# Halo and weight loads in pieces, and a second PSUM bank for the input transposes, in a dilated causal convolution

## The chip, the cores and the metric

The kernel runs on one core of a Trainium2 chip. The metric is the device time of one execution in microseconds (us). An execution has two numbers: its measured time, and the span of the profile (first to last instruction), which is shorter by about 1.75 us in the kernel before and by about 2.0 us in the changed kernel. Positions inside a kernel are given in us from the start of the span.

Names: the matrix engine is PE (PEld is its weight load), VectorE is DVE, ScalarE is ACT, GpSimd is POOL, the engine that issues transfers is SP. PSUM is the memory that the matrix engine writes its results to (`ps` in the profiles); the kernel uses it as eight banks. Copying a result out of it is called an eviction here.

## The reference

```python
B, T, D, K = 2, 16000, 144, 15            # x: B,T,D   w: K,D,2D   w_o: D,D   bf16
dil = 2; pad = (K - 1) * dil
xp = jnp.pad(x, ((0, 0), (pad, 0), (0, 0)))
h = sum over i of einsum('btc,cd->btd', xp[:, pad - i*dil : pad - i*dil + T, :], w[i])   # condensed
f, g = h[..., :D], h[..., D:]
return (tanh(f) * sigmoid(g)) @ w_o
```

It is a causal convolution with 15 taps at a distance of 2, a gate, and a projection.

## The kernel before

Each of the 128 partitions holds 125 consecutive time steps of one batch, plus a halo of 30 earlier rows that belong to the partition before it. Transposes on the matrix engine bring the channels onto the partitions, ScalarE copies them out of PSUM into a ring (`RX`), and VectorE forms three sums and differences per row (`RM`), from which two output rows are made together with fewer products. The transformed weights (`FW`) are made on the chip too. A main loop of 126 pairs of rows follows. The parts that the change and the argument touch are these:

```python
XTP = PS[:, 4, :].bitcast(BF16).rearrange("p (t h c) -> p t h c", t=4, h=2)   # one PSUM bank

def load_x_halo(b):                       # 30 rows, one piece: 112 + 15 partitions; row 0 is zero
    # ...
    S.add("pool", lambda e: [e.memset(XN[0:1, 0:HALO, :], 0.0)], writes=[("xn", "hz")], name="halo_z")
    S.add("sp", lambda e: [e.dma_start(XN[1:113, 0:HALO, :], xv[b][0:112, J - HALO:J, :])],
          writes=[("xn", "h0")], dma=k0, name="halo0")
    S.add("sp", lambda e: [e.dma_start(XN[113:128, 0:HALO, :], xv[b][112:127, J - HALO:J, :])],
          writes=[("xn", "h1")], dma=k1, name="halo1")
# ... compact(): POOL copies the last 16 channels of the rows into XRP

def op_prep(b, tq):                       # one group of four rows
    # PE: four transposes of XN into XTP, and from the fourth group on four of XRP ("packed rows")
    S.add("pe", emit_tx, reads=rk, writes=[("xtp",)], name="tx")
    # ACT: copy XTP to RX; the next group's transposes wait for it
    S.add("act", emit_cx, reads=[("xtp",)], writes=wk, name="cx")
    # DVE: three operations RX -> RM, one for each of the sums and differences
    # ...

def weight_transforms():                  # ten, three matmuls each, PSUM banks 0 to 3 in turn
    # PE: MB[bank] = I W[3q] +- I W[3q+1] + I W[3q+2]
    # ACT: FW[sgn, q] = 0.5 * MB[bank]
    # ...

load_halo_and_compact(0)
load_chunk_and_compact(0, 0)              # 8 rows
load_weights()                            # W (15 taps), 15 small pieces, w_o
for ci in range(1, NCH):
    load_chunk_and_compact(0, ci)
# ...
for n in init_tq:                         # nine groups
    op_prep(n // NTQ, n % NTQ)
weight_transforms()
for s in range(NP + 2):                   # main loop
    # ...
```

Of the kernel before, what the change touches and what calls it, by code (L numbers as in the profile page):

```python
# [122 lines left out]
def build_kernel(nc, x, w, w_o, out):  # L123
# [30 lines left out]
    r = HALO  # L154
    seq = [8, 16, 32]
    i = 0
    while r < NR:
        s = seq[i] if i < len(seq) else 40
        s = min(s, NR - r)
        chunks.append((r, r + s))  # L160
        r += s
        i += 1
    NCH = len(chunks)

    with ExitStack() as es:
# [22 lines left out]
        n_in_sems = 3 + B * (NCH + 2)  # L188
# [17 lines left out]
        XTP = PS[:, 4, :].bitcast(BF16).rearrange("p (t h c) -> p t h c", t=4, h=2)  # L206
# [23 lines left out]
        def load_x_halo(b):  # L230
            k0 = new_in_slot()
            k1 = new_in_slot()
            S.add("pool", lambda e: [e.memset(XN[0:1, 0:HALO, :], 0.0)], writes=[("xn", "hz")], name="halo_z")
            S.add("sp", lambda e: [e.dma_start(XN[1:113, 0:HALO, :], xv[b][0:112, J - HALO:J, :])],
                  writes=[("xn", "h0")], dma=k0, name="halo0")
            S.add("sp", lambda e: [e.dma_start(XN[113:128, 0:HALO, :], xv[b][112:127, J - HALO:J, :])],
                  writes=[("xn", "h1")], dma=k1, name="halo1")

# [10 lines left out]
        def load_x_chunk(b, ci):  # L249
            lo, hi = chunks[ci]  # L250
            k = new_in_slot()
            S.add("sp", lambda e: [e.dma_start(XN[:, lo:hi, :], xv[b][:, lo - HALO:hi - HALO, :])],
                  writes=[("xn", ci)], dma=k, name="xchunk")

        def load_weights():
            k = new_in_slot()
            S.add("sp", lambda e: [e.dma_start(W[:], w[:, 0:DM, :].rearrange("k c d -> c k d"))],
                  writes=[("w",)], dma=k, name="w")
            k2 = new_in_slot()
            wl = []  # L260
            for q in range(2):
                for g in range(NGP):
                    tap = q * NGP + (NGP - 1 - g)
                    if tap < K:
                        wl.append((q, g, tap))

            def emit_wg(e):
                return [e.dma_start(WG[g * DR:(g + 1) * DR, 0, q, :], w[tap, DM:D, :]) for (q, g, tap) in wl]
            S.add("sp", emit_wg, writes=[("wg", q, g) for (q, g, tap) in wl], dma=k2, ndma=len(wl), name="wg")
            k3 = new_in_slot()  # L270
            S.add("sp", lambda e: [e.dma_start(WO[:, 0, :], w_o[0:DM, :]),
                                   e.dma_start(WO[DM - DR:DM, 1, :], w_o[DM:D, :])],
                  writes=[("wo",)], dma=k3, ndma=2, name="wo")

        def xn_keys(lo, hi):
            ks = []
            if lo < HALO:
                ks += [("xn", "hz"), ("xn", "h0"), ("xn", "h1")]
            for ci, (a, c) in enumerate(chunks):
                if a < hi and lo < c:  # L280
                    ks.append(("xn", ci))
            return ks

        def xr_keys(b, rows):
            ks = set()
            for r_ in rows:
                if r_ < HALO:
                    ks.add(("xr", b, "h", r_ % 2))
                else:
                    for ci, (a, c) in enumerate(chunks):  # L290
                        if a <= r_ < c:
                            ks.add(("xr", b, ci, r_ % 2))
            return sorted(ks, key=str)

        def load_halo_and_compact(b):
            load_x_halo(b)
            compact(b, 0, HALO, xn_keys(0, HALO), "h")

        def load_chunk_and_compact(b, ci):
            load_x_chunk(b, ci)  # L300
            lo, hi = chunks[ci]
            compact(b, lo, hi, [("xn", ci)], ci)

        def weight_transforms():
            outs = []
            for q in range(NQ):
                for sgn in range(2):
                    outs.append((sgn, q))
            for n_, (sgn, q) in enumerate(outs):
                bank = n_ % 4  # L310

                def emit(e, sgn=sgn, q=q, bank=bank):
                    ins = []
                    for k in range(3):
                        idm = IDENT[:, 1, :] if (sgn == 1 and k == 1) else IDENT[:, 0, :]
                        ins.append(e.matmul(MB[bank], lhsT=idm, rhs=W[:, 3 * q + k, :], start=(k == 0), stop=(k == 2)))  # L316
                    return ins
                S.add("pe", emit, reads=[("ident", 0), ("ident", 1), ("w",)], writes=[("mb", bank)], name="wt")
                S.add("act", (lambda sgn=sgn, q=q, bank=bank: lambda e: [e.activation(  # L319
                    out=FW[:, sgn, q, :], in_=MB[bank], func=ACTF.Copy, scale=0.5)])(),  # L320
                    reads=[("mb", bank)], writes=[("fw", sgn, q)], name="wt_ev")
            S.add("act", lambda e: [e.activation(out=WG[:, 1, :, :], in_=WG[:, 0, :, :], func=ACTF.Copy, scale=-1.0)],
                  reads=[("wg", q, g) for q in range(2) for g in range(NGP)], writes=[("wgn",)], name="wgn")
# [4 lines left out]
        def op_prep(b, tq):  # L328
# [6 lines left out]
            sx = g0 % RSX  # L335
            rows_main = [jj0 + t + HALO for t in range(nt)]
# [17 lines left out]
            S.add("pe", emit_tx, reads=rk, writes=[("xtp",)], name="tx")  # L354
# [14 lines left out]
            S.add("act", emit_cx, reads=[("xtp",)], writes=wk, name="cx")  # L369
# [63 lines left out]
        def op_mm(b, ja, gi):  # L433
# [26 lines left out]
            if gi >= 2:  # L460
                rk.append(("w",))
# [115 lines left out]

        load_halo_and_compact(0)
        load_chunk_and_compact(0, 0)
        load_weights()  # L580
        for ci in range(1, NCH):
            load_chunk_and_compact(0, ci)
# [34 lines left out]
        for b in range(1, B):  # L617
            last_read = dict()
            for n in range(NTQT):
                if n // NTQ != b - 1 or firstneed[n] >= NP:  # L620
                    continue
                lo, hi = rows_of_tq(n)
                for key in xn_keys(lo, hi):
                    last_read[key] = max(0, stx[n])
            DELAY = 4
            halo_pi = max(last_read.get(("xn", "hz"), 0), last_read.get(("xn", "h0"), 0)) + DELAY
            loads_at.setdefault(halo_pi, []).append((b, "h"))
            for ci in range(NCH):
                pi = max(last_read.get(("xn", ci), 0) + DELAY, halo_pi)
                loads_at.setdefault(min(pi, NP - 1), []).append((b, ci))  # L630

        for n in init_tq:
            op_prep(n // NTQ, n % NTQ)
            flush_t(100)
        weight_transforms()

        for s in range(NP + 2):
# [3 lines left out]
            if s < NP:  # L641
                for (b, what) in loads_at.get(s, []):
                    if what == "h":
                        load_halo_and_compact(b)
                    else:
                        load_chunk_and_compact(b, what)
# [110 lines left out]
```

## Time and profile before

| | before |
|---|---|
| median time (13 executions) | 496.29 us |
| span of the profiled execution | 495.1 us |
| first transpose | 8.15 us |
| first main matmul (line L466) | 29.80 us |
| from there to the end | 465.3 us |

These lines are from the page of the kernel before: busy time with its share of the span and instruction count, then the chain of work that ended last, by engine.

```profile
PE 473.9 (96%) x4650; PEld 394.5 (80%) x4650; DVE 328.2 (66%) x866; ACT 320.7 (65%) x721; POOL 16.6 (3%) x36
...
PE 95%; ACT 2%; DMA 1%; issue 0%; DVE 0%; SPq 0%; DVEq 0%
```

The matrix engine is the bound. The next fence asks for busy time by stage (the ending is left out); the columns are the stretch, its length, then busy us of each engine with its number of instructions, the granted clock, and the transfer engines' share and rate.

```profile
0.00:8.15 8.15, 0.00 (x1) 0.04 (x2) 0.00 (x0) 1.28 (x1) 5.16 (x11) 1.00 0.78 187
8.15:23.64 15.49, 7.75 (x61) 5.70 (x61) 7.43 (x20) 6.82 (x8) 2.34 (x8) 1.00 0.76 249
23.64:29.80 6.16, 5.94 (x32) 3.84 (x31) 1.24 (x4) 4.62 (x11) 1.96 (x5) 1.00 1.00 385
29.80:488.00 458.20, 458.20 (x4543) 383.80 (x4544) 318.47 (x841) 305.39 (x696) 7.13 (x13) 1.00 0.09 32
```

From 29.80 to 488 us the matrix engine is busy for 458.20 of 458.20 us. Nothing can be won there without taking work from it. Before that there is a prologue of 29.80 us in which it is half idle. The granted clock in these records reads 1.00 here even where matmuls are twice as far apart as later, so the spacing has to be read from the instructions, not from that column.

The prologue in order of time, for the matrix engine (start, length, engine, line, operation, count, and in brackets the idle time before it and what ended it):

```profile
8.15 0.58 PE L348 MATMUL ps<-ident,xn 128*128 128x128 bf16 x4 [8.15 <-DMA xn<-in_x_dram]
9.41 0.61 PE L348 MATMUL ps<-ident,xn 128*128 128x128 bf16 x4 [0.68 <-ACT rx L361]
...
12.07 0.27 PE L348 MATMUL ps<-ident,xn 128*128 128x128 bf16 x1 [0.77 <-ACT rx L361]
...
14.19 0.29 PE L348 MATMUL ps<-ident,xn 128*128 128x128 bf16 x1 [1.10 <-ACT rx L360]
...
23.64 5.94 PE L316 MATMUL ps<-w_sb,ident 128*128 128x288 bf16 x30
29.80 1.39 PE L466 MATMUL ps<-fw_sb,rm 128*128 128x288 bf16 x10 [0.22 <-ACT fw_sb L319]
```

The brackets tell the story: after the halo has landed, each group waits for ScalarE's copy of the group before (0.68 us between small groups, 1.10 between those with packed rows). L348 and L351 are the transposes, L316 the weight transforms. The chain of waits shows the same ping-pong, one step at a time:

```profile
13.12 1.02 ACT rx L360
...
14.19 0.29 PE ps L348
...
15.26 1.02 ACT rx L360
...
28.15 1.52 ACT fw_sb L319 x4
```

It ends in ScalarE's queue of evictions (L319).

### The profile page before, as it was taken

What the parts mean: (1) busy time and instruction counts of PE and PEld (TensorE: products, weight loads), DVE (VectorE), ACT (ScalarE), POOL (GpSimd) and SP (SyncE); (2) the same over time, 40 slices, a digit from 0 to 9 for tenths busy, and PEclk for the clock granted to TensorE, in tenths of its full rate; (3) what the DMA queues carried; (4) which work ended last, traced back from release to release, by engine and by line L of the source; (5) the groups of instructions that cost most, each with busy time, mean ns of one, the idle gap of its engine ahead of it and who ended that gap; (6) DMA issues with size and microseconds to landing.
All of it is one profiled execution on the core that took longest, in us unless ns stands there. A gap on an engine that the chain in (4) does not pass through costs nothing.

```text
span 495.1 us, 11433 instructions
## 1 busy us (share of the span) xinstructions
PE 473.9 (96%) x4650; PEld 394.5 (80%) x4650; DVE 328.2 (66%) x866; ACT 320.7 (65%) x721; POOL 16.6 (3%) x36
## 2 busy tenths in 40 slices
PE   1599999999999999999999999999999999999995
PEld 1478888888888888888888888888888888888884
DVE  1546766676676676886776766766766676676663
ACT  2476666666666666776776666666666666666654
POOL 5150000000000000000000000000000000000000
PEclk9999999999999999999999999999999999999998
DMA  8760020000300000303000000000000000000001
GB/s 208 263 208 3 25 73 25 26 25 1 121 26 25 25 25 24 122 24 113 24 26 15 26 2 25 25 26 25 25 25 3 25 25 25 26 25 8 19 26 39
DMA packets 9008, 22.64 MB, mean 46 GB/s; under 512 B 1166, under 2 KB 3582, under 8 KB 7934
## 3 DMA queue, kind: packets, MB, share of 16 engines
q1 hardware_dynamic: 8956, 21.92, 13.1%
q8 instruction: 36, 0.59, 0.5%
q14 instruction: 16, 0.13, 0.1%
HBM read 12.70 MB, written 9.22 MB: 44 GB/s over the span
## 4 chain that ended last, share of the span: by engine, by line
PE 95%; ACT 2%; DMA 1%; issue 0%; DVE 0%; SPq 0%; DVEq 0%
PE ps L466 75%; PE ps L348 4%; PE ps L351 3%; PE ps L528 3%; PE ps L529 3%; PE ps L502 3%; PE ps L503 3%; DMA xn<-in_x_dram 1%; ACT rx L360 1%; PE ps L316 1%; ACT rx L361 0%; ACT fw_sb L319 0%; ACT zt L506 0%; DVE y L485 0%; ACT sg L489 0%
## 5 line engine op out<-in xcount | busy, mean ns | idle before, releaser
L466 PE MATMUL ps<-w_sb,rm 128*128 128x288 bf16 x1260 | 195.6, 286 | 0.0
L466 PE MATMUL ps<-fw_sb,rm 128*128 128x288 bf16 x1260 | 186.1, 286 | 0.2 <-ACT fw_sb L319 0.2
L466 PEld LDWEIGHTS ps<-w_sb,rm 128*128 128x128 bf16 x1260 | 123.3, 98 | 31.1
L466 PEld LDWEIGHTS ps<-fw_sb,rm 128*128 128x128 bf16 x1260 | 120.3, 98 | 28.1 <-issue 0.5
L489 ACT ACTIVATE sg<-y 128x288 bf16<-128x288 f32 x126 | 55.8, 443 | 99.3 <-DVE y L485 99.3
L506 ACT COPY zt<-ps 128x512 bf16<-128x512 bf16 x126 | 73.9, 586 | 55.1 <-PE ps L503 55.0
L466 PE MATMUL ps<-wg_sb,rx 128*128 128x288 bf16 x504 | 103.0, 286 | 0.0
L401 DVE TENSOR_TENSOR rm<-rx 128x512 bf16<-128x512 bf16 (+2 forms) x236 | 89.0, 408 | 17.0 <-ACT rx L361 10.9
L495 DVE TENSOR_TENSOR z<-tf,sg 128x288 bf16<-128x288 bf16 x126 | 38.8, 308 | 83.1 <-ACT tf L491 83.1
L485 DVE TENSOR_TENSOR y<-pq,ps 128x288 f32<-128x288 f32 x126 | 57.3, 454 | 46.3 <-PE ps L466 45.9
L360 ACT COPY rx<-ps 128x1024 bf16<-128x1024 bf16 x72 | 71.7, 996 | 6.9 <-PE ps L351 6.9
L475 DVE TENSOR_TENSOR pq<-s,ps 128x288 f32<-128x288 f32 x126 | 57.3, 455 | 12.3 <-PE ps L466 6.4
L348 PE MATMUL ps<-ident,xn 128*128 128x128 bf16 x306 | 44.4, 229 | 15.9 <-DMA xn<-in_x_dram 8.1
L481 DVE TENSOR_TENSOR y<-pq,ps 128x288 f32<-128x288 f32 x126 | 56.9, 451 | 3.6
L477 DVE TENSOR_TENSOR pq<-s,ps 128x288 f32<-128x288 f32 x126 | 56.4, 448 | 0.0
L491 ACT ACTIVATE tf<-y 128x288 bf16<-128x288 f32 x126 | 53.7, 426 | 0.0
L536 ACT CAST outb<-ps 128x288 bf16<-128x288 f32 x124 | 50.1, 404 | 0.0
L466 PEld LDWEIGHTS ps<-wg_sb,rx 128*128 128x128 bf16 x504 | 44.9, 98 | 6.3
L471 ACT COPY s<-ps 128x288 f32<-128x288 f32 x126 | 47.8, 379 | 0.0
L348 PEld LDWEIGHTS ps<-ident,xn 128*128 128x128 bf16 x306 | 30.5, 102 | 19.7 <-issue 9.1
L528 PE MATMUL ps<-wo_sb,zt 128*128 128x144 bf16 x252 | 44.3, 226 | 0.7 <-ACT outb L536 0.7
L529 PE MATMUL ps<-wo_sb,zt 128*128 128x144 bf16 x252 | 44.3, 226 | 0.0
(27 smaller groups left out, 290.4 us busy)
## 6 DMA issues: line engine op xcount, KB each, us to landing
out_dram<-outb SPq DMA_DIRECT2D x30, 288.0 KB, 2.1
xn<-in_x_dram SPq DMA_DIRECT2D x2, 1440.0 KB, 7.9
xn<-in_x_dram SPq DMA_DIRECT2D x2, 1152.0 KB, 5.9
xn<-in_x_dram SPq DMA_DIRECT2D x2, 1044.0 KB, 8.4
xn<-in_x_dram SPq DMA_DIRECT2D x2, 945.0 KB, 9.8
xn<-in_x_dram SPq DMA_DIRECT2D x2, 576.0 KB, 4.0
w_sb<-in_w_dram SPq DMA_DIRECT2D x1, 1080.0 KB, 10.1
xn<-in_x_dram SPq DMA_DIRECT2D x2, 288.0 KB, 8.2
```

The costliest lines, as they stand in the source:

```text
L348: ins.append(e.transpose(XTP[:, t, 0, :], XN[:, r_, 0:DM], IDENT[:, 0, :]))
L360: return [e.copy(out=RX[:, sx:sx + nt, :, :], in_=XTP[:, 0:nt, :, :])]
L401: S.add("dve", lambda e: [e.tensor_tensor(out=dst, in0=i0, in1=i1, op=op)], reads=rk_, writes=wk_, name="xf")
L466: ins.append(e.matmul(MB[bank], lhsT=l, rhs=r_, start=(ii == 0), stop=(ii == len(mms) - 1)))
L475: S.add("dve", lambda e: [e.tensor_tensor(out=PQ[:, sb, 0, :], in0=S2[:, sb, :], in1=MB[1], op=ADD)], reads=[("s2", sb), ("mb", 1)], write ...
L477: S.add("dve", lambda e: [e.tensor_tensor(out=PQ[:, sb, 1, :], in0=S2[:, sb, :], in1=MB[1], op=SUB)], reads=[("s2", sb), ("mb", 1)], write ...
L481: S.add("dve", lambda e: [e.tensor_tensor(out=Y[:, sb, 0, :], in0=PQ[:, sb, 0, :], in1=MB[2], op=ADD)], reads=[("pq", sb, 0), ("mb", 2)], ...
L485: S.add("dve", lambda e: [e.tensor_tensor(out=Y[:, sb, 1, :], in0=PQ[:, sb, 1, :], in1=MB[3], op=SUB)], reads=[("pq", sb, 1), ("mb", 3)], ...
L489: S.add("act", lambda e: [e.activation(out=SG[:, sb, :, :], in_=Y[:, sb, :, D:D2], func=ACTF.Sigmoid)], reads=[("y", sb, 0), ("y", sb, 1)] ...
L506: S.add("act", lambda e: [e.copy(out=ZT[:, sb, :, :], in_=ZTP[:, :, :])], reads=[("ztp",)], writes=[("zt", sb)], name="cz")
L528: ins.append(e.matmul(OP[:, t, :], lhsT=ZT[:, sb, 2 * t, :], rhs=WO[:, 0, :], start=True, stop=False))
L529: ins.append(e.matmul(OP[:, t, :], lhsT=ZT[:, sb, 2 * t + 1, :], rhs=WO[:, 1, :], start=False, stop=True))
```

## The change

The intent is to start earlier and to wait less: the first rows come in two pieces of 16 and 14 rows; the transposes get a second PSUM bank; the weights come in two loads (9 and 6 taps), so that six of the ten transforms stand between the seventh and the eighth group; and VectorE takes four of the ten evictions. VectorE also fills row 0 of the second piece with zeros.

```diff
+    while r < HALO:
+        s = min(16, HALO - r)
+        chunks.append((r, r + s, True))
...
-        XTP = PS[:, 4, :].bitcast(BF16).rearrange(...)
+        XTPS = [PS[:, k, :].bitcast(BF16).rearrange(...) for k in (4, 7)]
...
+                S.add("pool" if ci % 2 == 0 else "dve", lambda e: [e.memset(XN[0:1, lo:hi, :], 0.0)], ...)
+                S.add("sp", ... XN[1:113, lo:hi, :] <- xv[b][0:112, J - HALO + lo:J - HALO + hi, :] ...)
+                S.add("sp", ... XN[113:128, lo:hi, :] <- xv[b][112:127, ...] ...)
...
+            xb = (b * NTQ + tq) % 2
+            XTP = XTPS[xb]
...
+            if bank < 2:
+                S.add("act", ... e.activation(out=FW[:, sgn, q, :], in_=MB[bank], func=ACTF.Copy, scale=0.5) ...)
+            else:
+                S.add("dve", ... e.tensor_scalar_mul(out=FW[:, sgn, q, :], in0=MB[bank], scalar1=0.5) ...)
...
+        WSPLIT = 9
+        order0 = list(range(0, NHP)) + [first_main, "w0", "w1", "wg"] + list(range(first_main + 1, NCH))
...
         for i_, n in enumerate(init_tq):
             op_prep(n // NTQ, n % NTQ)
+            if i_ == 6:
+                while nwt < nwt_first:        # six
+                    weight_transform(nwt)
+                    nwt += 1
```

More of the change, by code (lines that the diff above doesn't have):

```diff
@@ L153, in build_kernel @@
     chunks = []
-    r = HALO
+    r = 0
+    while r < HALO:
+        s = min(16, HALO - r)
+        chunks.append((r, r + s, True))
+        r += s
     seq = [8, 16, 32]
@@ L159, in build_kernel @@
         s = min(s, NR - r)
-        chunks.append((r, r + s))
+        chunks.append((r, r + s, False))
         r += s
@@ L163, in build_kernel @@
     NCH = len(chunks)
+    NHP = len([c for c in chunks if c[2]])
     with ExitStack() as es:
@@ L186, in build_kernel @@
         PS = es.enter_context(nc.psum_tensor("ps", [128, 8, 512], F32))
-        n_in_sems = 3 + B * (NCH + 2)
+        n_in_sems = 4 + B * (NCH + NHP)
         sem_in = [es.enter_context(nc.semaphore("in%d" % i)) for i in range(n_in_sems)]
@@ L205, in build_kernel @@
         MB = [PS[:, k, 0:D2] for k in range(4)]
-        XTP = PS[:, 4, :].bitcast(BF16).rearrange("p (t h c) -> p t h c", t=4, h=2)
+        XTPS = [PS[:, k, :].bitcast(BF16).rearrange("p (t h c) -> p t h c", t=4, h=2) for k in (4, 7)]
         ZTP = PS[:, 5, :].bitcast(BF16)[:, 0:512].rearrange("p (t c) -> p t c", t=4)
@@ L228, in build_kernel @@
         S.add("pool", lambda e: [e.memset(WO[0:DM - DR, 1, :], 0.0)], writes=[("woz",)], name="woz")
-        def load_x_halo(b):
-            k0 = new_in_slot()
-            k1 = new_in_slot()
-            S.add("pool", lambda e: [e.memset(XN[0:1, 0:HALO, :], 0.0)], writes=[("xn", "hz")], name="halo_z")
-            S.add("sp", lambda e: [e.dma_start(XN[1:113, 0:HALO, :], xv[b][0:112, J - HALO:J, :])],
-                  writes=[("xn", "h0")], dma=k0, name="halo0")
-            S.add("sp", lambda e: [e.dma_start(XN[113:128, 0:HALO, :], xv[b][112:127, J - HALO:J, :])],
-                  writes=[("xn", "h1")], dma=k1, name="halo1")
         def compact(b, lo, hi, rkeys, tag):
@@ L247, in compact, with load_piece, piece_keys, compact_piece @@
                     reads=rkeys, writes=[("xr", b, tag, k)], name="compact")
-        def load_x_chunk(b, ci):
-            lo, hi = chunks[ci]
-            k = new_in_slot()
-            S.add("sp", lambda e: [e.dma_start(XN[:, lo:hi, :], xv[b][:, lo - HALO:hi - HALO, :])],
-                  writes=[("xn", ci)], dma=k, name="xchunk")
+        def load_piece(b, ci):
+            lo, hi, is_halo = chunks[ci]
+            if is_halo:
+                k0 = new_in_slot()
+                k1 = new_in_slot()
+                S.add("pool" if ci % 2 == 0 else "dve", lambda e: [e.memset(XN[0:1, lo:hi, :], 0.0)],
+                      writes=[("xn", ci, "z")], name="halo_z")
+                S.add("sp", lambda e: [e.dma_start(XN[1:113, lo:hi, :], xv[b][0:112, J - HALO + lo:J - HALO + hi, :])],
+                      writes=[("xn", ci, 0)], dma=k0, name="halo0")
+                S.add("sp", lambda e: [e.dma_start(XN[113:128, lo:hi, :], xv[b][112:127, J - HALO + lo:J - HALO + hi, :])],
+                      writes=[("xn", ci, 1)], dma=k1, name="halo1")
+            else:
+                k = new_in_slot()
+                S.add("sp", lambda e: [e.dma_start(XN[:, lo:hi, :], xv[b][:, lo - HALO:hi - HALO, :])],
+                      writes=[("xn", ci, 0)], dma=k, name="xchunk")
+        def piece_keys(ci):
+            if chunks[ci][2]:
+                return [("xn", ci, "z"), ("xn", ci, 0), ("xn", ci, 1)]
+            return [("xn", ci, 0)]
+        def compact_piece(b, ci):
+            lo, hi, is_halo = chunks[ci]
+            compact(b, lo, hi, piece_keys(ci), ci)
         def load_weights():
-            k = new_in_slot()
-            S.add("sp", lambda e: [e.dma_start(W[:], w[:, 0:DM, :].rearrange("k c d -> c k d"))],
-                  writes=[("w",)], dma=k, name="w")
             k2 = new_in_slot()
@@ L276, in xn_keys @@
             ks = []
-            if lo < HALO:
-                ks += [("xn", "hz"), ("xn", "h0"), ("xn", "h1")]
-            for ci, (a, c) in enumerate(chunks):
+            for ci, (a, c, h_) in enumerate(chunks):
                 if a < hi and lo < c:
-                    ks.append(("xn", ci))
+                    ks += piece_keys(ci)
             return ks
@@ L286, in xr_keys @@
             for r_ in rows:
-                if r_ < HALO:
-                    ks.add(("xr", b, "h", r_ % 2))
-                else:
-                    for ci, (a, c) in enumerate(chunks):
-                        if a <= r_ < c:
-                            ks.add(("xr", b, ci, r_ % 2))
-            return sorted(ks, key=str)
-        def load_halo_and_compact(b):
-            load_x_halo(b)
-            compact(b, 0, HALO, xn_keys(0, HALO), "h")
-        def load_chunk_and_compact(b, ci):
-            load_x_chunk(b, ci)
-            lo, hi = chunks[ci]
-            compact(b, lo, hi, [("xn", ci)], ci)
@@ L304, in weight_transforms @@
-        def weight_transforms():
-            outs = []
-            for q in range(NQ):
-                for sgn in range(2):
-                    outs.append((sgn, q))
-            for n_, (sgn, q) in enumerate(outs):
-                bank = n_ % 4
-                def emit(e, sgn=sgn, q=q, bank=bank):
-                    ins = []
-                    for k in range(3):
-                        idm = IDENT[:, 1, :] if (sgn == 1 and k == 1) else IDENT[:, 0, :]
-                        ins.append(e.matmul(MB[bank], lhsT=idm, rhs=W[:, 3 * q + k, :], start=(k == 0), stop=(k == 2)))
-                    return ins
-                S.add("pe", emit, reads=[("ident", 0), ("ident", 1), ("w",)], writes=[("mb", bank)], name="wt")
-                S.add("act", (lambda sgn=sgn, q=q, bank=bank: lambda e: [e.activation(
-                    out=FW[:, sgn, q, :], in_=MB[bank], func=ACTF.Copy, scale=0.5)])(),
-                    reads=[("mb", bank)], writes=[("fw", sgn, q)], name="wt_ev")
+                for ci, (a, c, h_) in enumerate(chunks):
+                    if a <= r_ < c:
+                        ks.add(("xr", b, ci, r_ % 2))
@@ new lines, in xr_keys, with weight_transform, emit @@
+            return sorted(ks, key=str)
+        wt_list = []
+        for q in range(NQ):
+            for sgn in range(2):
+                wt_list.append((sgn, q))
+        def weight_transform(n_):
+            sgn, q = wt_list[n_]
+            bank = n_ % 4
+            def emit(e):
+                ins = []
+                for k in range(3):
+                    idm = IDENT[:, 1, :] if (sgn == 1 and k == 1) else IDENT[:, 0, :]
+                    ins.append(e.matmul(MB[bank], lhsT=idm, rhs=W[:, 3 * q + k, :], start=(k == 0), stop=(k == 2)))
+                return ins
+            S.add("pe", emit, reads=[("ident", 0), ("ident", 1), ("w", 0 if 3 * q + 2 < WSPLIT else 1)],
+                  writes=[("mb", bank)], name="wt")
+            if bank < 2:
+                S.add("act", lambda e: [e.activation(out=FW[:, sgn, q, :], in_=MB[bank], func=ACTF.Copy, scale=0.5)],
+                      reads=[("mb", bank)], writes=[("fw", sgn, q)], name="wt_ev")
+            else:
+                S.add("dve", lambda e: [e.tensor_scalar_mul(out=FW[:, sgn, q, :], in0=MB[bank], scalar1=0.5)],
+                      reads=[("mb", bank)], writes=[("fw", sgn, q)], name="wt_ev")
@@ L322, in weight_transforms, with negate_packed_weights @@
+        def negate_packed_weights():
             S.add("act", lambda e: [e.activation(out=WG[:, 1, :, :], in_=WG[:, 0, :, :], func=ACTF.Copy, scale=-1.0)],
@@ L353, in emit_tx @@
                 return ins
-            S.add("pe", emit_tx, reads=rk, writes=[("xtp",)], name="tx")
+            S.add("pe", emit_tx, reads=rk, writes=[("xtp", xb)], name="tx")
             flush_needed(b * NTQ + tq - RSX // 4 + 1)
@@ L368, in op_prep @@
                     rx_owner[(sx + t, 1)] = g0 + t
-            S.add("act", emit_cx, reads=[("xtp",)], writes=wk, name="cx")
+            S.add("act", emit_cx, reads=[("xtp", xb)], writes=wk, name="cx")
             def transform(h, ring, rslots, kind):
@@ L460, in op_mm @@
             if gi >= 2:
-                rk.append(("w",))
+                rk += [("w", 0), ("w", 1)]
             def emit(e):
@@ L576, in req_tq, with load_w @@
             return b * NTQ + (ja + 2 + HM) // 4
-        load_halo_and_compact(0)
-        load_chunk_and_compact(0, 0)
-        load_weights()
-        for ci in range(1, NCH):
-            load_chunk_and_compact(0, ci)
+        WSPLIT = 9
+        def load_w(hf):
+            k = new_in_slot()
+            t0, t1 = (0, WSPLIT) if hf == 0 else (WSPLIT, K)
+            S.add("sp", lambda e: [e.dma_start(W[:, t0:t1, :], w[t0:t1, 0:DM, :].rearrange("k c d -> c k d"))],
+                  writes=[("w", hf)], dma=k, name="w")
+        first_main = NHP
+        order0 = list(range(0, NHP)) + [first_main, "w0", "w1", "wg"] + list(range(first_main + 1, NCH))
+        for it in order0:
+            if it == "w0":
+                load_w(0)
+            elif it == "w1":
+                load_w(1)
+            elif it == "wg":
+                load_weights()
+            else:
+                load_piece(0, it)
+        for ci in range(NCH):
+            compact_piece(0, ci)
         NTQT = B * NTQ
@@ L622, in build_kernel @@
                 lo, hi = rows_of_tq(n)
-                for key in xn_keys(lo, hi):
-                    last_read[key] = max(0, stx[n])
+                for ci, (a_, c_, h_) in enumerate(chunks):
+                    if a_ < hi and lo < c_:
+                        last_read[ci] = max(0, stx[n])
             DELAY = 4
-            halo_pi = max(last_read.get(("xn", "hz"), 0), last_read.get(("xn", "h0"), 0)) + DELAY
-            loads_at.setdefault(halo_pi, []).append((b, "h"))
+            prev = 0
             for ci in range(NCH):
-                pi = max(last_read.get(("xn", ci), 0) + DELAY, halo_pi)
+                pi = max(last_read.get(ci, 0) + DELAY, prev)
+                prev = pi
                 loads_at.setdefault(min(pi, NP - 1), []).append((b, ci))
-        for n in init_tq:
+        nwt = 0
+        nwt_first = 2 * (WSPLIT // 3)
+        for i_, n in enumerate(init_tq):
             op_prep(n // NTQ, n % NTQ)
+            cur_iter[0] = 10 ** 6
             flush_t(100)
-        weight_transforms()
+            cur_iter[0] = -10 ** 6
+            if i_ == 6:
+                while nwt < nwt_first:
+                    weight_transform(nwt)
+                    nwt += 1
+        while nwt < len(wt_list):
+            weight_transform(nwt)
+            nwt += 1
+        negate_packed_weights()
         for s in range(NP + 2):
@@ L642, in build_kernel @@
                 for (b, what) in loads_at.get(s, []):
-                    if what == "h":
-                        load_halo_and_compact(b)
-                    else:
-                        load_chunk_and_compact(b, what)
+                    load_piece(b, what)
+                    compact_piece(b, what)
                 b, ja, va = pairs[s]
```

## The prediction

> **What bounds the kernel.** The matrix engine: 96% busy by the page, 95% of the chain of waits, and 100% busy at full clock from 36 to 488 us in the stage table. Its waits after 30 us add up to 2.7 us, at the end. So about 465.3 us (29.80 to 495.1) is a solid block that this change does not touch; only the prologue before the first main matmul at 29.80 can shrink.
>
> **The prologue before (timeline).** 8.15 us: the whole halo (1.1 MB) has landed. Nine transpose groups ping-pong with ScalarE through one PSUM bank: 1.28 us each for the first three, about 2.14 for the six with packed rows (1.01 matrix engine, then 1.01 copy). 23.6 us: 30 weight-transform matmuls in 5.9 us, mostly 240 ns apart, ScalarE evicting all ten (0.41 each). 29.80: first main matmul, behind the last eviction.
>
> **What the change does.**
> 1. Halo in two pieces. The halo's packets run from 1.8 to 6.8 us; half the bytes are there at 4.4; the semaphore trails the last packet by about 1.2. The first piece should release the matrix engine at about 6.0. The fourth group needs the second piece and its compaction on POOL: about 8.7 (before: 12.07).
> 2. Second transpose bank. Groups with packed rows are paced by ScalarE's copy, 1.05 us rather than 2.14. Groups 4 to 7: matrix engine done at about 12.8, last copy at 13.9 (VectorE's three ring operations, 1.10 a group, just keep step).
> 3. Weights split 9 and 6 taps; six transforms come between groups seven and eight. The first half should land by about 11: no wait. 18 matmuls: 4.3 us at 240 ns, 2.2 at 122. End: 15.3 to 17.0.
> 4. Two more groups, four transforms, evictions shared with VectorE. The tail is copy, copy (1.05 each), three ring operations (1.1), then VectorE's eviction of transform 7 (estimated 0.47 from its other 288-wide PSUM reads), which stands behind those: about 4.6 us after the first six transforms.
>
> First main matmul: 19.9 to 21.9, centre 20.7, so 9.1 us earlier. Extra costs (more load issues, chunk loads about 1.4 us later, a short VectorE fill in the loop) should stay off the path: chunk 1 is compacted at about 21.7 and needed at about 24. In the main loop the second bank buys nothing, as the matrix engine never waits there for ScalarE.
>
> The Trainium skill, "TensorE: Matmul & The Clock Gate", Part 1, says the array runs at half rate until a free-running window of about 3.4 us has been busy. The trace agrees: spacing halved about 5 us after dense work began at 22.8; the earlier transposes (40% issue) ran at 107 ns all along. Whether the denser new transposes (80%) warm it by 12 to 15 us, or only the transforms do, is most of my range.
>
> **Prediction: 487.3 us, 80% range 485.5 to 489.3.** Faster by over 2%: 0.30; within 2%: 0.69; slower by over 2%: 0.01.
>
> **What would show it.** First transpose at about 6.0, fourth group at 8.7, groups then 1.05 us apart; first transform at about 12.7 without a weight wait; first main matmul near 20.7, released by VectorE's eviction; from there to the end still 465.3 us, two pairs per 7.27.
>
> **What would make it wrong.** The pieces landing together: up to 2 us lost at the start, though the second piece governs anyway. The weight half landing after 13 us. A matrix engine still cold at 20 us, or cooled by the gap of about 2 us before the main loop: about 2 us. A wait for chunk 1 in the first pairs. Better than expected: an early warm clock and a shorter tail, giving 485.5.

## The result

The changed kernel took 487.91 us (median of 8 executions, 487.01 to 488.47) against 496.29 us before (13 executions). The ratio is 0.9829, 95% interval 0.9818 to 0.9839: faster, by less than 2%. A ratio is the mean time of one kernel's runs over that of the other's in the same rounds, so it is not quite the ratio of these medians. Executions over 1.5% slower than the fastest of the same kernel are left out of the means. The predicted time was 487.3 us.

| | before | after | predicted |
|---|---|---|---|
| median time | 496.29 | 487.91 | 487.3 |
| span of the profiled execution | 495.1 | 486.1 | |
| first transpose | 8.15 | 5.82 | 6.0 |
| fourth group (first with packed rows) | 12.07 | 8.91 | 8.7 |
| first weight transform | 23.64 | 12.79 | 12.7 |
| first main matmul | 29.80 | 20.15 | 20.7 |
| from there to the end | 465.3 | 465.95 | 465.3 |

The page of the changed kernel, the same two lines:

```profile
PE 471.3 (97%) x4650; PEld 393.3 (81%) x4650; DVE 331.3 (68%) x872; ACT 318.7 (66%) x717; POOL 15.5 (3%) x40
...
PE 96%; DMA 1%; DVE 1%; ACT 1%; SPq 0%; issue 0%; POOL 0%; POOLq 0%; DVEq 0%
```

The stages of the changed kernel, cut at its own first transpose, first transform, first main matmul and ending (left out):

```profile
0.00:5.82 5.82, 0.01 (x1) 0.04 (x2) 0.90 (x1) 1.28 (x1) 3.48 (x11) 1.00 0.68 189
5.82:12.79 6.97, 5.24 (x44) 4.31 (x45) 4.09 (x12) 4.25 (x6) 2.13 (x6) 1.00 0.86 213
12.79:20.15 7.36, 5.67 (x48) 4.17 (x47) 5.71 (x18) 5.88 (x11) 0.83 (x2) 1.00 0.60 189
20.15:479.10 458.95, 458.50 (x4543) 383.64 (x4544) 319.51 (x842) 304.77 (x694) 9.05 (x21) 1.00 0.11 40
```

The two middle stages, 8.15 to 29.80 us before, have shrunk from 21.65 to 14.33 us, and the first by 2.33 us. The loop stage is now busy for 458.50 of 458.95 us: there is a hole of 0.45 us that was not there before.

The matrix engine's prologue after:

```profile
5.82 1.01 PE L355 MATMUL ps<-ident,xn 128*128 128x128 bf16 x8 [5.82 <-DMA xn<-in_x_dram]
7.08 0.61 PE L355 MATMUL ps<-ident,xn 128*128 128x128 bf16 x4 [0.25 <-ACT rx L368]
8.91 0.29 PE L355 MATMUL ps<-ident,xn 128*128 128x128 bf16 x1 [1.23 <-POOL xrp L241]
...
11.05 0.29 PE L355 MATMUL ps<-ident,xn 128*128 128x128 bf16 x1 [0.25 <-ACT rx L367]
...
12.79 3.30 PE L315 MATMUL ps<-w_sb,ident 128*128 128x288 bf16 x18
...
16.82 1.63 PE L315 MATMUL ps<-w_sb,ident 128*128 128x288 bf16 x12
20.15 1.40 PE L473 MATMUL ps<-fw_sb,rm 128*128 128x288 bf16 x10 [1.69 <-DVE fw_sb L323]
```

The waits for ScalarE between groups have shrunk to 0.25 us (twice). Two new waits have come: 1.23 us for POOL's compaction (L241) of the second halo piece, and 1.69 us for VectorE's eviction (L323) before the first main matmul. The list of the matrix engine's waits (total us, times, longest) after 24 us finds the hole in the loop:

```profile
PE ps L509 <- DVE z L502: 2.2, 2, 1.8
PE ps L535 <- ACT outb L543: 0.7, 1, 0.7
```

One of the two waits for z is the 1.8 us at the very end, which the kernel before has too. The other, 0.45 us, is at 36.68 us. The timeline there, lines of VectorE, ScalarE and the matrix engine:

```profile
34.26 0.90 DVE L250 MEMSET xn<- 1x1008 uint32 x1
...
35.09 0.38 DVE L492 TENSOR_TENSOR y<-pq,ps 128x288 f32<-128x288 f32 x1
...
35.51 0.44 ACT L496 ACTIVATE sg<-y 128x288 bf16<-128x288 f32 x1 [1.54 <-DVE y L492]
35.86 0.43 ACT L498 ACTIVATE tf<-y 128x288 bf16<-128x288 f32 x1
...
36.32 0.31 DVE L502 TENSOR_TENSOR z<-tf,sg 128x288 bf16<-128x288 bf16 x1 [0.52 <-ACT tf L498]
...
36.68 0.23 PE L509 MATMUL ps<-ident,z 128*128 128x128 bf16 x1 [0.45 <-DVE z L502]
```

VectorE's fill of row 0 for the second batch (L250, 0.90 us) stands before y (L492), y is what the gate (L496, L498) waits for, and the transposes of z wait for that.

### The profile page after: what moved, and what is told of

Its sections match the earlier page's. It is cut to its first block, busy times and chain, and to the rows that moved or that the text cites. A ratio compares the mean times of both kernels' runs of the same rounds, so it can differ in the third digit from the quotient of the medians.

```text
span 486.1 us, 11443 instructions
## 1 busy us (share of the span) xinstructions
PE 471.3 (97%) x4650; PEld 393.3 (81%) x4650; DVE 331.3 (68%) x872; ACT 318.7 (66%) x717; POOL 15.5 (3%) x40
## 4 chain that ended last, share of the span: by engine, by line
PE 96%; DMA 1%; DVE 1%; ACT 1%; SPq 0%; issue 0%; POOL 0%; POOLq 0%; DVEq 0%
PE ps L473 76%; PE ps L355 3%; PE ps L358 3%; PE ps L535 3%; PE ps L536 3%; PE ps L509 3%; PE ps L510 3%; DMA xn<-in_x_dram 1%; PE ps L315 1%; DVE rm L408 0%; ACT rx L367 0%; DVE xn L250 0%; ACT sg L496 0%; POOL xrp L241 0%; DVE y L492 0%
## 5 line engine op out<-in xcount | busy, mean ns | idle before, releaser
L496 ACT ACTIVATE sg<-y 128x288 bf16<-128x288 f32 x126 | 55.8, 443 | 100.0 <-DVE y L492 100.0
L492 DVE TENSOR_TENSOR y<-pq,ps 128x288 f32<-128x288 f32 x126 | 57.2, 454 | 46.7 <-PE ps L473 46.4
L498 ACT ACTIVATE tf<-y 128x288 bf16<-128x288 f32 x126 | 53.7, 426 | 0.0
L355 PE MATMUL ps<-ident,xn 128*128 128x128 bf16 x306 | 43.3, 227 | 7.5 <-DMA xn<-in_x_dram 5.8
L509 PE MATMUL ps<-ident,z 128*128 128x128 bf16 x252 | 41.7, 219 | 2.2 <-DVE z L502 2.2
```

Source lines behind the costliest of these rows:

```text
L355: ins.append(e.transpose(XTP[:, t, 0, :], XN[:, r_, 0:DM], IDENT[:, 0, :]))
L492: S.add("dve", lambda e: [e.tensor_tensor(out=Y[:, sb, 1, :], in0=PQ[:, sb, 1, :], in1=MB[3], op=SUB)], reads=[("pq", sb, 1), ("mb", 3)], ...
L509: ins.append(e.transpose(ZTP[:, 2 * t, :], Z[:, sb, t, 0:DM], IDENT[:, 0, :]))
```

## The experiments

Twelve kernels ran, in three jobs of four, each timed in five rounds beside the kernel before. All gave correct results. Every job has its own runs of the kernel before, and its kernels ran on one chip (jobs 2 and 3 on the same one); kernels of one job are compared first. "Rest" is the span from the first main matmul on. The position of the first main matmul is from the profiled execution alone and moves by about a microsecond between executions, for two reasons that the profiles show: the first data land up to 0.5 us earlier or later, and the matmul spacing halves at another moment. The profiled execution of the kernel before was one of its slower ones (496.83 us).

| job | kernel | median us | ratio to before | first main matmul | rest |
|---|---|---|---|---|---|
| 1 | s1_bank | 486.66 | 0.9806 | 19.55 | 465.45 |
| 1 | s2_halo | 494.20 | 0.9962 | 27.44 | 465.96 |
| 1 | s3_weights | 495.65 | 0.9988 | 27.93 | 465.67 |
| 1 | m1_fill_pool | 486.49 | 0.9800 | 18.74 | 465.26 |
| 2 | l1_no_bank | 494.44 (five executions) | 0.9968 | (no usable profile) | |
| 2 | l2_no_halo | 487.48 | 0.9834 | 20.31 | 465.39 |
| 2 | l3_no_weights | 486.57 | 0.9813 | 18.54 | 465.96 |
| 2 | w1_warm | 486.36 | 0.9807 | 18.32 | 466.28 |
| 3 | r1_after | 486.89 | 0.9812 | 19.56 | 465.94 |
| 3 | r2_bank | 486.86 | 0.9813 | 20.90 | 465.20 |
| 3 | v2_tail | 486.08 | 0.9794 | 18.93 | 465.27 |
| 3 | v4_all | 484.22 | 0.9762 | 18.70 | 465.20 |

The 95% intervals of the ratios are about 0.0012 to 0.0018 wide on each side, that is 0.6 to 0.9 us of time.

My theory was that the single bank's ping-pong was the main loss and that the two other parts are worth little beside it. The rival was that the early halo and the moved weights carry the gain.

### s1_bank: the second bank alone

```diff
 # the changed kernel, with the halo in one piece and the weight part undone
-        s = min(16, HALO - r)
+        s = HALO - r
-        WSPLIT = 9            # two loads, six transforms early, four evictions on VectorE
+        WSPLIT = K            # one load, all ten transforms after the ninth group, ScalarE evicts all
```

> Kernel before plus the second transpose bank only (halo in one piece, one weight load, ten evictions on ScalarE, transforms after all nine groups). My theory, the single bank's ping-pong is what the prologue lost most on: first transpose still at 8.15, groups with packed rows 1.05 us apart, first main matmul at 20.7 to 23.2 us (before 29.80), so about 488 us, nearly the whole gain of the change. Rival, the early halo and the moved weights carry the gain: at least 3 us of the 8.4 us are missing, 491 us or more.

Measured: 486.66 us, ratio 0.9806 (0.9794 to 0.9819). The bank alone gives the whole gain, and my own expectation was still too low by 1.3 us: its first data landed earlier in this profile (7.79 us), and the spacing had halved by 14 us, so the first main matmul came at 19.55 instead of 20.7 at best. The rival fails. Its line of the matrix engine's timeline:

```profile
19.55 1.39 PE L473 MATMUL ps<-fw_sb,rm 128*128 128x288 bf16 x10 [0.22 <-ACT fw_sb L320]
```

### s2_halo and s3_weights: the two other parts alone

```diff
 # s2_halo: the changed kernel with one bank and the weight part undone
 # s3_weights: the changed kernel with one bank and the halo in one piece; for both:
-            xb = (b * NTQ + tq) % 2
+            xb = 0
```

> Kernel before plus the halo in two pieces only (one bank, weights as before). My theory: first transpose at 5.8, groups keep their 1.28 and 2.14 us, so everything comes 2.3 us earlier, first main matmul at 27.4, minus 0.45 us given back in the loop by VectorE's row fill: 494.4 us. Rival, the pieces carry the gain: below 492 us.

> Kernel before plus the weight part only: load split 9 and 6 taps, six transforms between groups seven and eight, evictions shared with VectorE (one bank, one halo piece). My theory: worth nearly nothing, since the two last groups still alternate with ScalarE behind the transforms; first main matmul at 28.8 to 30.3 us, 496.1 us. Rival, the interleaving hides transform work: 494 us or less.

Measured: 494.20 us and 495.65 us. In the profile of the early halo alone the first data landed 2.77 us earlier than before (5.38), and the transposes came earlier by as much. The 30 transform matmuls then took 6.34 us instead of 5.94, so the first main matmul came at 27.44, close to the 27.4 expected partly by luck. In the loop about 0.4 us is given back, as expected. The weight part alone is worth 0.5 us at the edge of the interval (ratio 0.9988, 0.9976 to 1.0000). The first main matmul at 27.93 in its profile looks like more, but its first data landed at 7.68 us, 0.47 us earlier than in the profile of the kernel before, which was a slow one; the times are the better measure, and all five lie between 495.35 and 496.02 us. Without the second bank neither part comes near the gain.

### l1_no_bank, l2_no_halo, l3_no_weights: one part taken out of the whole

```diff
 # l1_no_bank                                   # l2_no_halo
-            xb = (b * NTQ + tq) % 2            -        s = min(16, HALO - r)
+            xb = 0                             +        s = HALO - r
 # l3_no_weights: WSPLIT = K and the edits of s1_bank that go with it
```

> The changed kernel with one transpose bank (halo pieces and weight part kept). My theory: the ping-pong is back, groups with packed rows 2.14 us apart from 9.65 us on; first main matmul at about 27.2, 494.2 us: nearly the whole gain is lost. Rival: half of the gain or more stays, below 492 us.

> The changed kernel with the halo in one piece (bank and weight part kept). My theory: first transpose back at 8.15, but the fourth group only about 1 us later than in the changed kernel (about 9.9 instead of 8.91), since there the second piece governs it; first main matmul at 21.2, and no 0.45 us lost in the loop: 488.4 us. Rival, an early landing counts in full: 2.3 us lost, 490 us or more.

> The changed kernel with the weight part undone (one load, all ten transforms after the ninth group, ScalarE evicts all). My theory: the matrix engine has the transposes and transforms in another order, but ScalarE's and VectorE's work bounds both; first main matmul at 19.7 to 21 us (20.15 with the weight part), 487.5 to 488.8 us. Rival, the interleaving is worth something of its own: 489 us or more.

Measured: 494.44 (median of the five usual executions), 487.48 and 486.57 us. Without the bank all but 1.4 us of the gain (495.80 - 494.44) is lost. Without the halo pieces 0.6 us is lost against r1_after, a run of the whole change on the same chip in the next job, or 1.1 us by the ratios; 0.9834 and 0.9812 have intervals that overlap. Without the weight part nothing is lost. Both of the last came out faster than expected (487.48 instead of 488.4, and 486.57, below its range of 487.5 to 488.8). I had reckoned from the profile after; in l3_no_weights' profile the second piece was compacted 0.69 us earlier (fourth group at 8.22 instead of 8.91), and in l2_no_halo's the first 18 transform matmuls took 2.61 us instead of 3.30.

l1_no_bank had one execution of 1,770 us, and the profile is of that one. It is no evidence for the change: its matmuls are about four times as far apart as at full rate from the first transpose to the last instruction (see the last section). The other five executions took 493.86 to 495.07 us.

### r1_after and r2_bank: the whole change and the bank alone, side by side

```diff
 # r1_after: the changed kernel, no edit. r2_bank: the kernel of s1_bank, no edit.
```

> The changed kernel again, beside the second bank alone, on one chip, as their ratios to the kernel before (0.983 and 0.981) came from different jobs. My theory after eight runs: halo pieces and weight part add about 1 us of prologue to the bank and give 0.45 us back in the loop, so both are within 1 us of each other: 487.2 us here. The spread between executions (about 1.4 us) is the moment at which the array's rate doubles.

> Kernel before plus the second transpose bank alone, again, on the same chip as the whole change. My theory: 486.8 us, within 1 us of the whole change. Rival: the other two parts are worth their 2 us and 0.5 us, measured alone, also on top of the bank: then the whole change is at least 1.5 us faster than this.

Measured: 486.89 and 486.86 us, ratios 0.9812 and 0.9813. On one chip, in the same rounds, the whole change and its one part are equal within their intervals. So where did the 2 us of the early halo go, that s2_halo shows? The chain of waits of both tells. First the bank alone, its longest pieces:

```profile
1.25 6.56 DMA xn<-in_x_dram
...
7.95 0.60 PE ps L355 x4
...
18.14 2.62 ACT fw_sb L320 x7
...
20.90 1.14 PE ps L473 x8
```

Now the whole change:

```profile
2.15 5.33 DMA xn<-in_x_dram
...
7.63 0.86 POOL xrp L241 x2
8.54 0.29 PE ps L355
...
12.63 2.87 PE ps L315 x18
...
15.98 1.02 ACT rx L367
17.03 2.10 DVE rm L408 x6
19.13 0.38 DVE fw_sb L323
19.56 1.52 PE ps L473 x11
```

With the bank alone the chain starts at the one halo load and ends in ScalarE's evictions. In the whole change it no longer starts at the first piece, which released the matrix engine at 5.45, but at the second piece, which lands at about 7.5, and then at POOL's two copies of it (0.86 us); the matrix engine waits 1.23 us there. The second piece comes hardly earlier than the undivided halo (7.48 us here against 7.81 in r2_bank). At the end the chain runs through VectorE's six ring operations (2.10 us) and then VectorE's eviction behind them (0.38 us), which took the place of ScalarE's queue of evictions. The gain of the early landing became a wait for the second piece, and the moved weights traded one queue for another. The first main matmul still comes 1.3 us earlier than in this profile of r2_bank, but 0.8 us of that is r2_bank's slower transforms, 30 matmuls in 4.88 us against 4.07 us in s1_bank, the same kernel, whose first main matmul is at 19.55. The row fill takes another 0.45 us back.

One more loss lies outside the span. l3_no_weights and s1_bank differ in the halo pieces alone, though they ran in different jobs on different chips. With the pieces the first main matmul comes 1.0 us earlier (18.54 against 19.55), the rest takes 0.5 us longer, and the measured time exceeds the span by 2.0 instead of 1.75 us. Of the whole, 0.2 us is left in the profiled executions (486.53 against 486.75 us). What the time outside the span is spent on is not shown. My theory of the spread is borne out in part: between r2_bank and s1_bank, one kernel, the moment at which the rate doubles is worth 0.8 us.

### m1_fill_pool: the row fill off VectorE

```diff
-                S.add("pool" if ci % 2 == 0 else "dve", lambda e: [e.memset(XN[0:1, lo:hi, :], 0.0)],
+                S.add("pool" if ci % 2 == 0 or b > 0 else "dve", lambda e: [e.memset(XN[0:1, lo:hi, :], 0.0)],
```

> The changed kernel with one edit: the second batch's fill of row 0 of the second halo piece stands on POOL, not VectorE. My theory, read from the trace: VectorE's 0.90 us fill at 34.26 delays the gate chain and the matrix engine waits 0.45 us at 36.7 for z. That wait goes; prologue unchanged; 487.4 us. Rival, the wait is due to the POOL compactions beside it and stays: 487.9 us.

Measured: 486.49 us. The wait is gone: this is the list of the matrix engine's waits in the loop of this kernel, with only the one at the end left for z.

```profile
PE ps L509 <- DVE z L502: 1.8, 1, 1.8
...
```

From the first main matmul to the end it takes 465.26 us. Over the kernels with the fill on VectorE that stretch is 465.94 to 466.28 us, over those without it 465.20 to 465.67. The second wait for z stands in the list of every usable profile with the fill on VectorE and in none without it. So the fill is the cause, and the compactions beside it, which are still there, are not. The time is 0.9 us better than expected; as the whole change itself took 486.89 us in a later job, that excess need not be the fill's. The fill's own worth is read from the trace, not from the times, whose intervals overlap.

### w1_warm: a full-rate matrix engine from the start

```diff
+        NWARM = 40        # PE: 40 matmuls of the identity with itself into an idle bank, result unused
```

> The changed kernel with 40 dummy 128-wide matmuls on the identity before the first transpose (result thrown away). My theory of the clock: matmul spacing halves only after the dense work that starts at 8.9 has run some 5 us; 40 dummies fill about 4.3 us from 1.8 on, so the array is at full rate by 5.8 or soon after, and 8 of the 18 first transforms lose 0.12 us each: first main matmul about 0.9 us earlier, 487.0 us. Rival, ScalarE and VectorE bound the prologue and a faster array gains nothing: 487.9 us.

Measured: 486.36 us, ratio 0.9807 (0.9793 to 0.9822). The mechanism is there in the profiled execution, with transposes 56 ns apart rather than 107 from 7.07 us on, and the first main matmul at 18.32 us. The gain against r1_after (same chip, next job) is 0.5 us, within the intervals, so the size stays open.

```profile
1.53 4.45 PE L659 MATMUL ps<-ident 128*128 128x128 bf16 x40 [1.53 <-POOL ident L221]
...
7.07 0.40 PE L355 MATMUL ps<-ident,xn 128*128 128x128 bf16 x4 [0.45 <-ACT rx L368]
8.57 0.23 PE L355 MATMUL ps<-ident,xn 128*128 128x128 bf16 x1 [1.10 <-POOL xrp L241]
...
10.29 0.23 PE L355 MATMUL ps<-ident,xn 128*128 128x128 bf16 x1 [0.66 <-ACT rx L367]
```

A matmul here takes 0.22 us from start to modelled end; the starts, 8.57, 8.63, 8.69 and on, show the spacing. What ScalarE still sets are the gaps of 0.66 and 0.29 us.

### v2_tail and v4_all: a version meant to beat both

```diff
 # v2_tail: the row fill as in m1_fill_pool, and
-                for kind in range(3):
+                for kind in (1, 2, 0):                 # the first main matmuls need kind 1, then 2
-        nwt_first = 2 * (WSPLIT // 3)                  # six transforms ahead of group eight
+        nwt_first = 4
+            if i_ == len(init_tq) - 1:
+                while nwt < len(wt_list):
+                    if wt_list[nwt] in ((0, 3), (1, 3)):   # VectorE's two late evictions
+                        flush_t(1)                         # one ring operation ahead of each
+                    weight_transform(nwt)
+                    nwt += 1
 # v4_all: v2_tail, and
+        NWARM = 34
+        # first batch, second halo piece: one of the two compactions on ScalarE
```

> A version meant to beat both: the changed kernel, fill of row 0 on POOL, ring operations in the order the first matmuls need them, four instead of six transforms ahead of group eight, and VectorE's last two evictions placed between the ring operations. My theory, that the tail behind the last copies (ring operations and then VectorE's eviction, 1.7 us of waiting) holds the first main matmul: it starts about 1.2 us earlier, and the 0.45 us wait in the loop goes; 485.8 us. Rival, the tail is bounded by ScalarE's copies and evictions: 487.0 us.

> As v2_tail, plus 34 dummy matmuls ahead of the first transpose so that the array is at full rate when the data come, and one of the two compactions of the second halo piece on ScalarE, which is idle then. Expected: fourth group 0.4 us earlier, transforms all at about 122 ns, less spread between executions; 485.0 us. If the array's rate does not matter behind ScalarE's pace: as v2_tail.

Measured: 486.08 and 484.22 us. v2_tail is 0.8 us faster than r1_after beside it, with intervals that just overlap; its first main matmul no longer waits for VectorE but 0.22 us for ScalarE's eviction, so the first main matmul came 0.6 us earlier and then met the next queue. It missed its 485.8 us by 0.3 us. v4_all is faster than everything: ratio 0.9762 (0.9748 to 0.9776) against 0.9812 (0.9798 to 0.9825) for the change in the same rounds, with intervals clear of each other. That is 2.4% below the kernel before.

Why it is that much faster is only partly shown. Its executions fall into two groups: 484.09, 484.18 and 484.22 us, and 485.41 and 485.81 us. The profile is of the slowest, and there the 34 dummy matmuls had not helped: eight transposes still took 1.01 us at 5.88, and the twelve transform matmuls that began at 12.55 took 2.24 us.

```profile
5.88 1.01 PE L356 MATMUL ps<-ident,xn 128*128 128x128 bf16 x8 [0.53 <-DMA xn<-in_x_dram]
7.14 0.61 PE L356 MATMUL ps<-ident,xn 128*128 128x128 bf16 x4 [0.25 <-ACT rx L369]
8.70 0.26 PE L356 MATMUL ps<-ident,xn 128*128 128x128 bf16 x1 [0.95 <-ACT xrp L242]
```

That the three faster ones are those in which the spacing had halved in time fits w1_warm's profile, but no profile of them exists. The compaction on ScalarE gave little: from the start of the second piece's compaction to the fourth group took 0.62 us here (8.08 to 8.70) and 0.76 in v2_tail (7.76 to 8.52), not 0.4 us less.

## Why the prediction was right, and where it was not

The time was 487.91 us against 487.3 predicted, inside the range of 485.5 to 489.3, and within 2%, the class given most.

- **The bound.** "About 465.3 us is a solid block": it took 465.95 us. The 0.65 us more includes the 0.45 us hole. The prediction had the fill in its list of things that "should stay off the path". That step was wrong: the fill took 0.90 us on VectorE, at the place where y waits behind it. m1_fill_pool shows it.
- **The halo in pieces.** First transpose 6.0 predicted, 5.82 measured; fourth group 8.7 against 8.91. The compaction of the second piece was slow: 0.86 us for its two copies in r1_after's chain, with VectorE's ring operations beside it. The Trainium skill, "GPSIMD Engine Reference", in its specification table, says GpSimd's SBUF interfaces are shared with VectorE, with contention when VectorE reads two SBUF inputs. The traces agree: in s2_halo, where with one bank the ring operations begin only at 7.90, the same two copies took 0.51 us (7.39 to 7.90). So the second bank, which brings the ring operations forward, itself lengthens the wait for the second piece, by 0.2 to 0.4 us over the profiles (0.71 to 0.92 us for the two copies); the prediction did not name that. The argument "the second piece governs anyway" was right, and is one reason why the halo part is worth little on top of the bank; the wait in the loop and the time outside the span are the others.
- **The second bank.** Groups 1.05 us apart predicted; ScalarE's copies of groups four to seven ran in pairs 2.14 us apart (9.98 and 12.12), 1.07 per group. "In the main loop the second bank buys nothing" held: 465.45 and 465.20 us with the bank alone. The Trainium skill, "PSUM — Partial Sum Buffer", summary of rules, advises a different bank when PSUM is read while a matmul runs, and a semaphore for each bank. With one bank the wait on that semaphore is the ping-pong, and the second bank is the whole of the gain, 9.5 us in s1_bank and r2_bank. What counts may be the second buffer rather than the second bank: a group with packed rows fills a bank (128x1024 bf16), and smaller groups in two halves of one bank were not tried.
- **The weights.** First transform at 12.79 without a weight wait, as predicted. The prediction did not say what this part is worth. It is worth nothing measurable on top of the bank and the halo pieces (l3_no_weights 0.9813, r1_after 0.9812).
- **The tail.** 4.6 us from the end of the first six transforms to the first main matmul predicted, about 4.2 measured (the next transpose starts at 15.93, the first main matmul at 20.15), and the releaser was VectorE's eviction as predicted.
- **The clock.** The Trainium skill, "TensorE: Matmul & The Clock Gate", Part 1, puts the doubling of the rate at about 4 us of sustained work, with the moment set by a free-running window. The traces agree in kind: the same 18 transform matmuls took 3.30 us in the profiled execution after, 3.08 in r1_after and 2.56 in m1_fill_pool. Their starts are about 240 ns apart before the doubling and 122 after it, and in the profile after they change at 14.7 us, after eight of the 18. The denser transposes counted toward the warming, as the middle of the range had assumed: in m1_fill_pool the spacing had halved by 12.1 us, before the first transform matmul. With one bank and sparse transposes (s3_weights) the same 18 took 4.28 us. But the moment is not set by the program alone: in two executions of the bank alone, on two chips, it came between 13.4 and 14.0 us (s1_bank) and at 17.9 (r2_bank).
- **Issues of loads.** "Chunk loads about 1.4 us later" was wrong and did not matter: the first was issued 0.86 us later (2.63 instead of 1.77), the next ones at 15.39 us, and at 15.72 before, because the 15 small weight loads took 10.18 us to issue instead of 12.10.

The total was right partly by luck. In the profiled executions the first main matmul came 9.65 us earlier, where 9.1 was predicted, the rest took 0.65 us longer and the time outside the span 0.25 us longer, where no change was predicted. These errors cancel in part.

A right total also hid a wrong picture of the parts in one respect: the prediction summed the three parts along one chain and never asked what each would be worth alone. The runs show, from the medians of one job, 9.5 us for the bank, 2.0 for the halo and 0.5 for the weights, each alone, and 8.4 us (first result) to 9.5 us (r1_after) for all three together.

## What to carry to other kernels

When two engines alternate through one PSUM bank in a prologue, give them a second bank first, and only then look at loads: the step that was paced by the sum of both engines is paced by the slower one. A load cut into pieces is worth only as much as the work that the first piece alone can feed; find out which piece the chain of waits starts from afterwards. A small fill or copy put on an engine with a third of its time free can still cost half its length if it stands in front of the operation that a full engine will wait for.

## What the Trainium skill lacked or had wrong

- "TensorE: Matmul & The Clock Gate", Part 1, does not say how dense "sustained" work must be. Here transposes that filled 40% of the time (eight in 0.86 us of every 2.14) ran at 107 ns for over 10 us and never warmed the array, while in m1_fill_pool 32 of them in the 3.85 us from 8.27 on, nearly 90% of the time, ended with the spacing halved at about 12.1 us.
- The same page gives a warm-up budget of about 3.4 us. Here it took longer: 40 dummy matmuls begun at 1.53 us, followed at once by transposes, ran at half rate until about 6.2 us in the profiled execution of w1_warm (4.7 us), and 34 of them (3.81 us) and a gap of 0.53 us had not halved the spacing in that of v4_all. In r2_bank it halved 8.7 us after the denser transposes began (9.21 to 17.9). The free-running window would make the moment vary; no run tests that it is the reason.
- The same page, in its caveats, tells of the rate being stuck at a quarter for over 50 us. One execution of l1_no_bank (1,770 us) had 128-column transposes 210 ns apart from 10 us to the end of 1,768 us, where 56 ns is normal, while the granted clock in the records read 1.00. The other five executions of that kernel were normal; what set it off stays open.
- "GPSIMD Engine Reference" names the contention with VectorE but gives no size; here two POOL copies of 128 x 112 took 0.86 us beside VectorE's two-input operations (r1_after) and 0.51 without them (s2_halo).
- No page that I read gives the cost of a fill on GpSimd: on a single partition 1 x 2304 bf16 elements took 2.01 us and 1 x 4320 took 3.69 us.
